# Column sums of a weight, on their way through memory: four small transfers from GpSimd's queue to SyncE's, and the operations around them

## The chip, the core and the metric

One core of one Trainium2 chip runs the whole program. The metric is the device time in microseconds (us) of one launch. Three runs of the kernel before the change gave 235.82, 237.19 and 238.05; the median is 237.19. A profile is one more execution, taken by the hardware profiler; its times are in us from the start of its span unless they are marked ns.

## What is computed

A layer norm of x, then an attention with a sliding dilated window and a gated MLP side by side, all added to x. S = 2048 rows, D = 512, 32 heads of 16, a window of 8 rows at a distance of 2, F = 1792 (two halves of 896).

```python
xn   = layernorm(x)                                  # 2048 x 512
q, k, v = split(xn @ wqkv)                           # 32 heads of 16
logits  = q . k[pos - 2*w] * scale,  w = 0..7        # masked where pos - 2*w < 0
attn    = softmax(logits)
A = (sum over w of attn * v[pos - 2*w]) @ wo
z  = gelu(xn @ w_in)
z1 = z[:, :896];  z2 = layernorm(z[:, 896:])
B  = (z1 * (w_sp @ z2 + b_sp[:, None])) @ w_out
out = x + A + B
```

## The kernel before

x comes in 16 blocks of 128 rows. Each block is normalised on VectorE and transposed by DMA into xnT. TensorE then makes V, Q, K, the second half z2 and the first half z1T of the MLP, later the product of w_sp with z2 (L976, the largest part, in four quarters of 112 matmuls), and at the end the outputs (L1032 with wo, L1041 with w_out). ScalarE moves results out of PSUM, with gelu and exp. VectorE makes the window products of Q and K (L743, with their sums L748), the softmax, the products of the attention with V (the "PV" blocks, L1004 and L1007) and the gate (L987 adds the bias, L990 multiplies).

**The three uncorrected blocks.** To let TensorE start early, V of the blocks 0 to 2 is computed from x that is not centred (`NRAW = 3`). Such a V block needs a correction: minus the mean times rstd, times the column sums of the weight wv. The column sums are made on TensorE with ones (L777, in the step that also reduces the logits of the first two quarters, "red0", L766) and come as four partial sums on four groups of 32 partitions. To add them up and to spread them over 128 partitions they go through memory, in `colsum` (L657 to L672):

- ScalarE copies the partial sums out of PSUM, negated ("cse", L658),
- transfer csa (L660) writes the four rows of 512 to DRAM,
- transfer csb (L662) reads them back, four columns to a partition,
- GpSimd adds them in two steps, csu and csv (L665, L667),
- transfer csc (L669) writes the 512 sums to DRAM,
- transfer csr (L671) reads them into all 128 partitions.

All four transfers are issued by GpSimd. Then VectorE corrects the three blocks (`fix_all`, L753, "the corrections"), and GpSimd's queue stores them to the scratch memory vscr (L686), from which the PV blocks are loaded (L999).

**The order of the work.** Every operation is given to a planner (`Plan.schedule`) with an estimated duration, a priority and what it reads and writes. The planner simulates the engines and fixes each engine's order of instructions. Of the operations that can start within a window of `tol` ns after the first one that can, it takes the one of the highest priority. For some transfers it takes a landing time from a table (`land`) in place of an estimate. Lists of names (L1072 to L1082) pin the order of some operations; a pair of names on one queue fixes which of the two goes first. On the chip each engine runs its list in order and waits at semaphores, so what stands behind a waiting instruction waits as well.

**Space.** Many tensors lie over each other in the arena. Before the change the column sums (ncs) and their partial sums (csp) share one place inside z1T; the raw V blocks (vraw) and the corrected ones (Vn0) lie in z1T as well. A z1 group whose place is still in use is evacuated from PSUM (L882) only when that use is over. The bias of w_sp's product (bbc) shares its place with four slots of V blocks. The third quarter of w_sp's transposes (wT2, L949) lies over the window products, and so waits for the second reduction of the logits ("red2", L766 again).

**Other names in the text.** L789 adds the mask to the logits on VectorE. L849 to L862 normalise z2 in four waves of four blocks; in each, GpSimd takes a power (zr0 to zr3, L859), which VectorE's four L862 wait for. In the order of the lists, zr2 stands behind csa and zr3 behind csr. SyncE loads w_out (L954), wo in four parts (L958; each part waits until the one before it has landed), the bias (L941), and x for the residual (L1022, read by L1047).

Of the kernel before, what the change touches and what calls it, by code (L numbers as in the profile page):

```python
# [9 lines left out]
F32 = mybir.dt.float32  # L10
ALU = mybir.AluOpType
ACTF = mybir.ActivationFunctionType
# [334 lines left out]
def build_kernel(nc, A_x, A_wqkv, A_wo, B_x, B_w_in, B_w_sp, B_b_sp, B_w_out, out, report=False, emit=True):  # L347
    S = A_x.shape[1]
    D = A_x.shape[2]
    assert D == 512 and S % 512 == 0  # L350
    NB = S // 128
# [8 lines left out]
    NRAW = 3  # L360
# [5 lines left out]
    cpart = nc.dram_tensor("cpart", (4, 512), F32).ap()  # L366
    cscr = nc.dram_tensor("cscr", (512,), F32).ap()


    off = {}  # L370
# [19 lines left out]
        place((n + 1) & ~1, **{name: 0})  # L390
    off["xn"] = off["attn"]
    off["xcT"] = off["pb"] + 4096
    off["Vn0"] = off["z1T"] + 1536
    off["ncs"] = off["z1T"] + 3 * S + 1024
    off["vraw"] = off["ncs"] + S
    AR = top[0]
    NWS = 3

    foff = {}
    fb = 0  # L400
    for name, n in (("prime", 4), ("mx", 128), ("Zb", 256), ("Z", 128), ("maskt", 128), ("st6", NB * 6),
                    ("mv", NB * 2), ("vpe", NB), ("rstd", NB), ("s1", NB), ("s2", NB), ("m2", NB), ("msq", NB), ("mr", 4), ("csq", 16), ("css", 4),
                    ("vpe2", NB), ("rstd2", NB), ("mhalf", 4)):
        foff[name] = fb
        fb += n
# [3 lines left out]
    plan = Plan()  # L409

    with ExitStack() as es:
        ar = es.enter_context(nc.sbuf_tensor("arena", [128, AR], BF))
        fp = es.enter_context(nc.sbuf_tensor("fpool", [128, FR], F32))
# [3 lines left out]
        def A(name, n, o2_=0):  # L417
            return ar[:, off[name] + o2_: off[name] + o2_ + n]
# [4 lines left out]
        def Fv(name, n, o2_=0):  # L423
            return fp[:, foff[name] + o2_: foff[name] + o2_ + n]
# [4 lines left out]
        def PC(o_, dims):  # L429
            return bass.AP(tensor=ps, offset=o_, ap=[[PR, 128]] + [list(d) for d in dims])  # L430
# [6 lines left out]
        def R1(key, name, n, o_=0):  # L437
            R(key, "sb", [(off[name] + o_, off[name] + o_ + n)])
# [44 lines left out]
                R1(("xcT", b, hf), "xcT", 256, 512 * b + 256 * hf)  # L483
            R(("xnT", 0, hf), "sb", [(off["xnT"] + dc * S, off["xnT"] + dc * S + 128) for dc in (2 * hf, 2 * hf + 1)])
        R1("ncs", "ncs", 1024)
        for b in range(NRAW):
            R1(("Vn", "raw", b), "Vn0", 512, S * b)
        R1("csp", "ncs", 1024)
        for fc in range(FC):
            for j in range(NJ):  # L490
                R1(("z1T", fc, j), "z1T", 512, fc * S + 512 * j)
# [11 lines left out]
        def c_act(n, psum=True, accum=False):  # L503
            return (170.0 if psum else 205.0) + n * 0.833 + (200.0 if accum else 0.0)
# [7 lines left out]
        T = plan.add  # L512

        def dma(eng, fn, nbytes, chan, reads=(), writes=(), name="", xbar=False, prio=0.0, after=()):
            return T(eng, fn, reads=reads, writes=writes, name=name, prio=prio, after=after,
                     dma=dict(chan=chan, nbytes=nbytes, xbar=xbar, iss=(1270.0 if nbytes < 400000 else 2200.0) if xbar else None))
# [7 lines left out]
        ncs = A("ncs", 1024).bitcast(F32)  # L524
# [5 lines left out]
          writes=["ident"], est=300, name="ident1")  # L530
# [124 lines left out]
            return AC(off["xnT"] + dc * S + 128 * b, [[1, 128]])  # L655

        def colsum(bk):  # L657
            T("act", lambda a: a.activation(ncs.rearrange("p (d h) -> p d h", d=16), PC(bk.col(), [[1, 16], [16, 32]]), ACTF.Copy, scale=-1.0), reads=[bk], writes=["csp"], est=c_act(512),  # L658
              name="cse", prio=-0.5)
            dma("pool", lambda e: e.dma_start(cpart, A("ncs", 1024).bitcast(F32)[0:128:32, :]),  # L660
                8192, "csa", reads=["csp"], writes=["cpart"], name="csa", prio=-5)
            dma("pool", lambda e: e.dma_start(Fv("csq", 16).rearrange("p (q i) -> p q i", q=4),  # L662
                                              bass.AP(tensor=cpart.tensor, offset=cpart.offset, ap=[[4, 128], [512, 4], [1, 4]])),
                8192, "csb", reads=["cpart"], writes=["csq"], name="csb", prio=-5)
            T("pool", lambda g: g.tensor_tensor(Fv("csq", 8), Fv("csq", 8), Fv("csq", 8, 8), ALU.add), writes=["csq"],  # L665
              est=200, name="csu", prio=-5)
            T("pool", lambda g: g.tensor_tensor(Fv("css", 4), Fv("csq", 4), Fv("csq", 4, 4), ALU.add), reads=["csq"],  # L667
              writes=["css"], est=200, name="csv", prio=-5)
            dma("pool", lambda e: e.dma_start(bass.AP(tensor=cscr.tensor, offset=cscr.offset, ap=[[4, 128], [1, 4]]), Fv("css", 4)),  # L669
                2048, "csc", reads=["css"], writes=["cscr"], name="csc", prio=-5)  # L670
            dma("pool", lambda e: e.dma_start(ncs, bass.AP(tensor=cscr.tensor, offset=cscr.offset, ap=[[0, 128], [1, 512]])),  # L671
                128 * 2048, "csr", reads=["cscr"], writes=["ncs"], name="csr", prio=-5)  # L672

        def vraw(b):
            return A("vraw", 1024, S * b).bitcast(F32)
# [13 lines left out]
        def v_block(b):  # L689
            bk = plan.bank("V%d" % b)  # L690
            sl = b % 8
            vk = ("Vn", "raw", b) if b < NRAW else ("Vn", sl)
            vn = A("Vn0", 512, S * b) if b < NRAW else A("Vn" if sl < 4 else "bbc", 512, 512 * (sl % 4))

            for hf in range(2):
                def mm(t, hf=hf):
                    last = None
                    for dc in (2 * hf, 2 * hf + 1):
                        last = t.matmul(P(bk, 512), A("xcT", 128, 512 * b + 128 * dc) if b < NRAW else xTv(b, dc),  # L699
                                        A("wv", 512, 512 * dc), start=(dc == 0), stop=(dc == 3))  # L700
                    return last
                T("pe", mm, reads=[("xcT", b, hf) if b < NRAW else ("xnT", b), ("wv", hf)], writes=[bk],
                  est=2 * c_mm(512) , name="V%d_%d" % (b, hf), prio=(2 if b < 4 else 60 + b))
            vdh = vn.rearrange("p (d h) -> p d h", d=16)
            if b < NRAW:
                T("act", lambda a: a.activation(vraw(b).rearrange("p (d h) -> p d h", d=16), PC(bk.col(), [[1, 16], [16, 32]]), ACTF.Copy,
                                                   scale=Fv("rstd", 1, b)),
                  reads=[bk, ("rstd", b)], writes=[("vraw", b)], est=c_act(512), name="Ve%d" % b, prio=4)
                fixes.append((b, vn, vk))
                return  # L710
            else:
                T("act", lambda a: a.activation(vdh, PC(bk.col(), [[1, 16], [16, 32]]), ACTF.Copy),  # L712
                  reads=[bk], writes=[vk], est=c_act(512), name="Ve%d" % b, prio=4)
            v_write(b, vn, vk)
# [357 lines left out]
        for names in (["warm%d" % wi for wi in range(NWARM)] +  # L1072
                      ["xTx0a", "xTx0b", "warm%d" % NWARM, "V0_0", "xTx1", "V0_1", "xTx2", "V1_0", "V1_1", "xTr0", "V2_0", "V2_1",
                       "z2_0_0", "z2_0_0b", "z2_0_1", "z2_1_0", "z2_1_1", "z2_2_0", "z2_2_1", "V3_0", "V3_1", "z2_3_0", "z2_3_1", "V4_0", "V4_1", "z2_4_0", "z2_4_1", "Q0_0", "Q0_1", "K0_0", "K0_1"],
                      ("rstd7", "Vw3"), ("csr", "Vw0", "Vw1", "Vw2"),
                      ("bnst0", "bnag0", "vpe0", "bnst1", "bnag1", "vpe1", "norm0", "bnst2", "norm1", "bnag2", "vpe2", "bnst3", "norm2",
                       "bnag3", "vpe3", "norm3", "bnst4", "bnag4", "vpe4", "mr", "norm4", "bnst5"),
                      ["bnst%d" % b for b in range(5, NB)],
                      ("xTc0_0", "xTc0_1", "xTc1_0", "xTc1_1", "xTc2_0", "xTe0_0", "xTe0_2", "Ve1", "Ve0", "Ve2",
                       "z2g0", "z2g1", "z2s0"), ("ldx4", "xTd1", "xTd2", "xTd3", "xTd4", "ldq", "ldk", "ldx5", "ldx6", "ldx7", "ldwin1", "ldx8"), ("ldx15", "xTd5"),  # L1080
                      *[("ldwin1", "ldx%d" % b) for b in range(9, NB)], *[("z2_4_1", "%s0_%d" % (n, c)) for n in "QK" for c in range(4)],
                      ("V10_1", "Q3_3"), ("csa", "zr2"), ("csr", "zr3")):  # L1082
            for n0, n1 in zip(names, names[1:]):
                if byname[n0] not in byname[n1].deps:
                    byname[n1].odeps.add(byname[n0])

        plan.schedule(tol=58.0, dma_bw=285.0, dma_lat=1600.0, overlap=60.0,
                      land=dict(ldx0=3600.0, ldwv0=4120.0, ldx1=4550.0, ldwv1=5230.0, ldx2=5600.0, ldwin2a=7650.0, ldx3=6050.0,
                                ldwin2b=8950.0, csa=77000.0, csb=80500.0, csc=83200.0, csr=85900.0, ldx4=9100.0, ldx5=18150.0, ldq=16300.0, xTd3=12130.0, ldk=17800.0, ldx6=18500.0, ldx7=18900.0, xTd4=13900.0, xTd1=9600.0, xTd2=10850.0, ldwin1=21500.0))
        if report:  # L1090
            print("arena", AR, "fp", FR)
            plan.report()
# [48 lines left out]
```

## Time and profile before

| | us |
|---|---|
| median of three runs | 237.19 |
| the profiled execution, its own time | 237.73 |
| its span, first to last instruction | 236.5 |
| ScalarE busy, TensorE's granted clock | 95.9, 1.000 |
| the last L748 on VectorE | 118.82 to 121.11 |
| last matmul ends (L1041) | 234.6 |

The longest waits that concern the change, as the view of waits gives them (who waited, for whom, total, times, longest):

```profile
POOL fpool L665 <- DMA fpool<-cpart: 4.3, 1, 4.3
...
POOL vscr L686 <- DVE arena L753: 3.3, 1, 3.3
...
DVE arena L753 <- DMA arena<-cscr: 2.9, 1, 2.9
...
POOL arena L671 <- DMA cscr<-fpool: 1.4, 1, 1.4
PE ps L766 <- DVE arena L748: 1.4, 1, 1.4
ACT arena L882 <- DVE arena L753: 1.3, 1, 1.3
```

A line of a timeline gives the start, the length, the engine, the line of the kernel, the operation, what it writes and reads with its shape, and how often it stands there in a row. In brackets is the time for which the engine was idle before it, and what ended that. DVE is VectorE, ACT ScalarE, PE TensorE, POOL GpSimd, SP SyncE. A wait is a loss only where the engine that sets the end had nothing else to do; matmuls are pipelined, so the lengths of TensorE's groups overlap a little.

### The profile page before, as it was taken

To read this page: it belongs to the slowest core of one execution; us is meant where nothing else is said; L and a number is where in the kernel's file an instruction comes from. 1 tells how busy PE (TensorE), PEld (TensorE's weight loads), DVE (VectorE), ACT (ScalarE), POOL (GpSimd) and SP (SyncE) were. 2 spreads that over 40 slices of the span, in tenths; PEclk is the share of its full clock that TensorE was granted. 3 is DMA by queue.
4 is the path that set the end of the run, shared out by engine and by line. 5 is a ranking of instruction groups with operands and counts; after the bars stand their busy time and mean duration, and the time that the engine had idled before them with its cause. 6 is when DMAs were issued, how large, how long until landed. Compare 5 with 4: busy or idle time off the path is not lost.

```text
span 236.5 us, 3005 instructions
## 1 busy us (share of the span) xinstructions
PE 232.0 (98%) x1127; PEld 108.3 (46%) x1127; DVE 207.2 (88%) x271; ACT 95.9 (41%) x143; POOL 33.4 (14%) x62
## 2 busy tenths in 40 slices
PE   8999999999999999999979999999999999999996
PEld 3455455544544444444434444444444444444443
DVE  4706999999998987999999999999798999999932
ACT  4798778888986587611010162111111111000000
POOL 2305740504206263000000000000000000000000
DMA  6769935999764523017089999999999692893552
GB/s 198 223 198 369 175 87 117 229 208 186 194 200 144 128 54 103 3 44 215 7 281 276 197 300 237 202 208 314 269 275 244 186 336 56 285 297 81 180 163 67
DMA packets 83823, 44.55 MB, mean 188 GB/s; under 512 B 56060, under 2 KB 83100, under 8 KB 83808
## 3 DMA queue, kind: packets, MB, share of 16 engines
q1 hardware_dynamic: 82400, 41.66, 68.5%
q0 software_dynamic: 976, 2.40, 3.9%
q10 hardware_dynamic: 432, 0.30, 0.4%
q8 instruction: 9, 0.15, 0.3%
q14 instruction: 6, 0.05, 0.1%
HBM read 26.62 MB, written 4.22 MB: 130 GB/s over the span
## 4 chain that ended last, share of the span: by engine, by line
PE 74%; DVE 14%; DMA 8%; issue 2%; POOL 1%; ACT 1%; ACTq 0%
PE ps L976 31%; PE ps L1041 10%; PE ps L830 10%; PE ps L722 9%; PE ps L1032 6%; PE ps L699 5%; DVE arena L748 4%; DVE arena L743 4%; PE ps L876 3%; DMA fpool<-cpart 2%; DMA arena<-cscr 2%; DMA cpart<-arena 1%; DMA arena<-arena 1%; DMA arena<-in_A_x_dram 1%; POOL fpool L667 1%
## 5 line engine op out<-in xcount | busy, mean ns | idle before, releaser
L976 PE MATMUL ps<-arena 128*128 128x512 bf16 x448 | 97.0, 379 | 0.0
L976 PEld LDWEIGHTS ps<-arena 128*128 128x128 bf16 x448 | 43.8, 98 | 53.0 <-issue 0.4
L984 ACT ACTIVATE arena<-ps 128x1024 bf16<-128x1024 f32 (+1 forms) x16 | 14.7, 917 | 80.9 <-PE ps L976 80.9
L743 DVE TENSOR_TENSOR arena<-arena 128x4096 bf16<-128x4096 bf16 x16 | 36.4, 2281 | 0.1
L1004 DVE TENSOR_TENSOR arena<-arena 128x4096 bf16<-128x4096 bf16 x16 | 36.5, 2284 | 0.0
L1007 DVE TENSOR_TENSOR arena<-arena 128x2048 bf16<-128x2048 bf16 (+1 forms) x32 | 30.1, 950 | 0.1
L722 PE MATMUL ps<-arena 128*128 128x512 bf16 x128 | 28.8, 379 | 0.0
L748 DVE TENSOR_TENSOR arena<-arena 128x4096 bf16<-128x4096 bf16 x12 | 27.5, 2288 | 0.1
L1041 PE MATMUL ps<-arena 128*128 128x512 bf16 (+2 forms) x119 | 27.0, 366 | 0.0
L830 PE MATMUL ps<-arena 128*128 128x448 bf16 x128 | 25.9, 353 | 0.2
L876 PE MATMUL ps<-arena 128*128 128x512 bf16 x112 | 24.7, 379 | 0.0
L722 PEld LDWEIGHTS ps<-arena 128*128 128x128 bf16 x128 | 14.4, 113 | 13.3 <-ACT arena L712 0.4
L731 ACT ACTIVATE arena<-ps 128x1024 bf16<-128x1024 f32 x16 | 16.3, 1022 | 6.7 <-PE ps L722 6.4
L830 PEld LDWEIGHTS ps<-arena 128*128 128x128 bf16 x128 | 12.4, 98 | 12.8 <-DMA arena<-in_B_w_in_dram 0.7
L1047 DVE TENSOR_TENSOR arena<-ps,arena 128x512 bf16<-128x512 f32 (+2 forms) x17 | 11.1, 656 | 7.2 <-PE ps L1041 7.1
L1041 PEld LDWEIGHTS ps<-arena 128*128 128x128 bf16 x119 | 11.4, 98 | 12.8
L876 PEld LDWEIGHTS ps<-arena 128*128 128x128 bf16 x112 | 10.9, 98 | 13.4 <-ACT arena L882 0.5
L1032 PE MATMUL ps<-arena 128*128 128x512 bf16 (+2 forms) x68 | 16.6, 366 | 0.0
L838 ACT ACTIVATE arena<-ps 128x896 bf16<-128x896 f32 x16 | 14.6, 913 | 3.9 <-PE ps L830 3.8
L699 PE MATMUL ps<-arena 128*128 128x512 bf16 x64 | 15.9, 379 | 0.2 <-ACT arena L630 0.2
L882 ACT ACTIVATE arena<-ps 128x1024 bf16<-128x1024 f32 (+1 forms) x16 | 13.9, 922 | 4.7 <-PE ps L876 3.4
L622 DVE BATCH_NORM_STATS2 fpool<-arena 128x6 f32<-128x512 bf16 x16 | 10.7, 679 | 5.5 <-DMA arena<-in_A_x_dram 5.5
(68 smaller groups left out, 171.0 us busy)
## 6 DMA issues: line engine op xcount, KB each, us to landing
arena<-vscr SPq DMA_DIRECT2D x16, 1024.0 KB, 6.2
arena<-in_A_x_dram SPq DMA_DIRECT2D x30, 128.0 KB, 4.3
vscr<-arena POOLq DMA_DIRECT2D x16, 128.0 KB, 3.7
out_dram<-arena SPq DMA_DIRECT2D x15, 128.0 KB, 2.0
arena<-in_A_wqkv_dram SPq DMA_DIRECT2D x2, 512.0 KB, 4.6
arena<-in_B_w_in_dram SPq DMA_DIRECT2D x2, 448.0 KB, 5.2
arena<-in_B_w_in_dram SPq DMA_DIRECT2D x1, 896.0 KB, 8.3
arena<-in_B_w_out_dram SPq DMA_DIRECT2D x1, 896.0 KB, 4.9
```

The source lines that it names most:

```text
L699: last = t.matmul(P(bk, 512), A("xcT", 128, 512 * b + 128 * dc) if b < NRAW else xTv(b, dc), A("wv", 512, 512 * dc), start=(dc == 0), stop ...
L722: last = t.matmul(P(bk, 512, 512 * which), AC(off["wqk"] + 2048 * which + 512 * dc + c, [[4, 128]]), AC(off["xnT"] + dc * S + 512 * j, [[1 ...
L731: T("act", lambda a: a.activation(AC(qo, [[ko - qo, 2], [1, 512]]), P(bk, 1024).rearrange("p (t n) -> p t n", t=2), ACTF.Copy, scale=0.5), ...
L743: T("dve", (lambda pbv, qb, kb: lambda v: v.tensor_tensor(pbv, qb, kb, ALU.mult))(pbv, qb, kb), reads=rd, writes=[("pb", s_)], est=c_tt(40 ...
L748: T("dve", (lambda av, bv: lambda v: v.tensor_tensor(av, av, bv, ALU.add))(av, bv), reads=[("pb", 1)], writes=[("pb", acc)], est=c_tt(4096 ...
L830: last = t.matmul(P(bk, 448, 512 * hf), xTv(b, dc), AC(off["w_in2"] + 896 * dc + 448 * hf, [[1, 448]]), start=(dc == 0), stop=(dc == 3))
L876: last = t.matmul(P(bk, 512, 512 * i), AC(off["w_in1"] + 896 * dc + 128 * fc, [[1, 128]]), AC(off["xnT"] + dc * S + 512 * j, [[1, 512]]), ...
L976: last = t.matmul(P(bk, 512, 512 * i), AC(off["z2"] + FH * sh + 128 * fc, [[1, 128]]), AC(off["wT%d" % r_] + sh * 512, [[1, 512]]), start= ...
L1004: T("dve", lambda v: v.tensor_tensor(tv, tv, av, ALU.mult), reads=[("attn", b)], writes=[("Vs", sv)], est=c_tt(4096), name="pv%d" % b, pri ...
L1007: T("dve", (lambda n: lambda v: v.tensor_tensor(A("Vs", n, 4096 * sv), A("Vs", n, 4096 * sv), A("Vs", n, 4096 * sv + n), ALU.add))(n), wri ...
L1032: last = t.matmul(P(bk, cn), AC(off["OT"] + 512 * tb + 128 * cc, [[1, 128]]), AC(off["wo"] + 512 * cc + c0, [[1, cn]]), start=(cc == 0), s ...
L1041: last = t.matmul(P(bk, cn), AC(off["z1T"] + fc * S + 128 * tb, [[1, 128]]), AC(off["w_out"] + 512 * fc + c0, [[1, cn]]), start=False, sto ...
```

## The change

The four transfers are issued by SyncE in place of GpSimd. csb and csc move pieces of 16 floats (64 bytes) on 32 partitions in place of 4 floats (16 bytes) on 128, so the two sums on GpSimd are of 32 and 16 elements on 32 partitions. In the pinned orders, SyncE's load of w_out comes behind csa, csb, csc and csr; the first part of wo and the first load of x for the residual come behind csr; zr3 comes behind csv in place of csr, and zr2 is no longer pinned. The sums now lie in the place of the bias, so the bias is loaded after the corrections. The partial sums keep a place in z1T; the corrected V blocks go to ordinary slots of Vn. The pinned order of the three blocks' stores is dropped. The planner's window is 4 ns in place of 58, and the table has new landing times for the four transfers.

```diff
-    off["Vn0"] = off["z1T"] + 1536
-    off["ncs"] = off["z1T"] + 3 * S + 1024
-    off["vraw"] = off["ncs"] + S
+    off["ncs"] = off["bbc"]
+    off["csp"] = off["z1T"] + 3 * S + 1024
+    off["vraw"] = off["csp"] + S
...
-            dma("pool", lambda e: e.dma_start(cpart, A("ncs", 1024).bitcast(F32)[0:128:32, :]),
+            dma("sp", lambda e: e.dma_start(cpart, A("csp", 1024).bitcast(F32)[0:128:32, :]),
                 8192, "csa", reads=["csp"], writes=["cpart"], name="csa", prio=-5)
-            dma("pool", lambda e: e.dma_start(Fv("csq", 16).rearrange("p (q i) -> p q i", q=4),
-                                              bass.AP(tensor=cpart.tensor, offset=cpart.offset, ap=[[4, 128], [512, 4], [1, 4]])),
+            dma("sp", lambda e: e.dma_start(csv(0, 64).rearrange("p (q i) -> p q i", q=4),
+                                            bass.AP(tensor=cpart.tensor, offset=cpart.offset, ap=[[16, 32], [512, 4], [1, 16]])),
                 8192, "csb", reads=["cpart"], writes=["csq"], name="csb", prio=-5)
-            T("pool", lambda g: g.tensor_tensor(Fv("csq", 8), Fv("csq", 8), Fv("csq", 8, 8), ALU.add), writes=["csq"],
-              est=200, name="csu", prio=-5)
+            T("pool", lambda g: g.tensor_tensor(csv(0, 32), csv(0, 32), csv(32, 32), ALU.add), writes=["csq"],
+              est=1200, name="csu", prio=-5)
...
-            dma("pool", lambda e: e.dma_start(bass.AP(tensor=cscr.tensor, offset=cscr.offset, ap=[[4, 128], [1, 4]]), Fv("css", 4)),
+            dma("sp", lambda e: e.dma_start(bass.AP(tensor=cscr.tensor, offset=cscr.offset, ap=[[16, 32], [1, 16]]), csv(64, 16)),
                 2048, "csc", reads=["css"], writes=["cscr"], name="csc", prio=-5)
-            dma("pool", lambda e: e.dma_start(ncs, bass.AP(tensor=cscr.tensor, offset=cscr.offset, ap=[[0, 128], [1, 512]])),
+            dma("sp", lambda e: e.dma_start(ncs, bass.AP(tensor=cscr.tensor, offset=cscr.offset, ap=[[0, 128], [1, 512]])),
                 128 * 2048, "csr", reads=["cscr"], writes=["ncs"], name="csr", prio=-5)
+
+        def csv(o_, n):
+            return fp[0:32, foff["csq"] + o_:foff["csq"] + o_ + n]
...
-            vk = ("Vn", "raw", b) if b < NRAW else ("Vn", sl)
-            vn = A("Vn0", 512, S * b) if b < NRAW else A("Vn" if sl < 4 else "bbc", 512, 512 * (sl % 4))
+            vk = ("Vn", sl)
+            vn = A("Vn" if sl < 4 else "bbc", 512, 512 * (sl % 4))
...
-                      ("rstd7", "Vw3"), ("csr", "Vw0", "Vw1", "Vw2"),
+                      ("rstd7", "Vw3"),
...
-                      ("V10_1", "Q3_3"), ("csa", "zr2"), ("csr", "zr3")):
+                      ("V10_1", "Q3_3"), ("csa", "csb", "csc", "csr", "ldwout"), ("csr", "ldwo0"), ("csr", "ldxr0"), ("csv", "zr3")):
...
-        plan.schedule(tol=58.0, dma_bw=285.0, dma_lat=1600.0, overlap=60.0,
+        plan.schedule(tol=4.0, dma_bw=285.0, dma_lat=1600.0, overlap=60.0,
...
-                                ldwin2b=8950.0, csa=77000.0, csb=80500.0, csc=83200.0, csr=85900.0, ldx4=9100.0,
+                                ldwin2b=8950.0, csa=75800.0, csb=78400.0, csc=83400.0, csr=86500.0, ldx4=9100.0,
```

More of the change, by code (lines that the diff above doesn't have):

```diff
@@ L401, in build_kernel @@
     for name, n in (("prime", 4), ("mx", 128), ("Zb", 256), ("Z", 128), ("maskt", 128), ("st6", NB * 6),
-                    ("mv", NB * 2), ("vpe", NB), ("rstd", NB), ("s1", NB), ("s2", NB), ("m2", NB), ("msq", NB), ("mr", 4), ("csq", 16), ("css", 4),
+                    ("mv", NB * 2), ("vpe", NB), ("rstd", NB), ("s1", NB), ("s2", NB), ("m2", NB), ("msq", NB), ("mr", 4), ("csq", 64), ("css", 16),
                     ("vpe2", NB), ("rstd2", NB), ("mhalf", 4)):
@@ L485, in build_kernel @@
         R1("ncs", "ncs", 1024)
-        for b in range(NRAW):
-            R1(("Vn", "raw", b), "Vn0", 512, S * b)
-        R1("csp", "ncs", 1024)
+        R1("csp", "csp", 1024)
         for fc in range(FC):
@@ L657, in colsum @@
         def colsum(bk):
-            T("act", lambda a: a.activation(ncs.rearrange("p (d h) -> p d h", d=16), PC(bk.col(), [[1, 16], [16, 32]]), ACTF.Copy, scale=-1.0), reads=[bk], writes=["csp"], est=c_act(512),
+            T("act", lambda a: a.activation(A("csp", 1024).bitcast(F32).rearrange("p (d h) -> p d h", d=16), PC(bk.col(), [[1, 16], [16, 32]]), ACTF.Copy, scale=-1.0), reads=[bk], writes=["csp"], est=c_act(512),
               name="cse", prio=-0.5)
-            dma("pool", lambda e: e.dma_start(cpart, A("ncs", 1024).bitcast(F32)[0:128:32, :]),
+            dma("sp", lambda e: e.dma_start(cpart, A("csp", 1024).bitcast(F32)[0:128:32, :]),
@@ L664, in colsum @@
                 8192, "csb", reads=["cpart"], writes=["csq"], name="csb", prio=-5)
-            T("pool", lambda g: g.tensor_tensor(Fv("csq", 8), Fv("csq", 8), Fv("csq", 8, 8), ALU.add), writes=["csq"],
-              est=200, name="csu", prio=-5)
-            T("pool", lambda g: g.tensor_tensor(Fv("css", 4), Fv("csq", 4), Fv("csq", 4, 4), ALU.add), reads=["csq"],
-              writes=["css"], est=200, name="csv", prio=-5)
-            dma("pool", lambda e: e.dma_start(bass.AP(tensor=cscr.tensor, offset=cscr.offset, ap=[[4, 128], [1, 4]]), Fv("css", 4)),
+            T("pool", lambda g: g.tensor_tensor(csv(0, 32), csv(0, 32), csv(32, 32), ALU.add), writes=["csq"],
+              est=1200, name="csu", prio=-5)
@@ L670, in colsum @@
+            T("pool", lambda g: g.tensor_tensor(csv(64, 16), csv(0, 16), csv(16, 16), ALU.add), reads=["csq"],
+              writes=["css"], est=1200, name="csv", prio=-5)
+            dma("sp", lambda e: e.dma_start(bass.AP(tensor=cscr.tensor, offset=cscr.offset, ap=[[16, 32], [1, 16]]), csv(64, 16)),
                 2048, "csc", reads=["css"], writes=["cscr"], name="csc", prio=-5)
-            dma("pool", lambda e: e.dma_start(ncs, bass.AP(tensor=cscr.tensor, offset=cscr.offset, ap=[[0, 128], [1, 512]])),
+            dma("sp", lambda e: e.dma_start(ncs, bass.AP(tensor=cscr.tensor, offset=cscr.offset, ap=[[0, 128], [1, 512]])),
@@ L1085, in build_kernel @@
                     byname[n1].odeps.add(byname[n0])
-        plan.schedule(tol=58.0, dma_bw=285.0, dma_lat=1600.0, overlap=60.0,
+        plan.schedule(tol=4.0, dma_bw=285.0, dma_lat=1600.0, overlap=60.0,
                       land=dict(ldx0=3600.0, ldwv0=4120.0, ldx1=4550.0, ldwv1=5230.0, ldx2=5600.0, ldwin2a=7650.0, ldx3=6050.0,
-                                ldwin2b=8950.0, csa=77000.0, csb=80500.0, csc=83200.0, csr=85900.0, ldx4=9100.0, ldx5=18150.0, ldq=16300.0, xTd3=12130.0, ldk=17800.0, ldx6=18500.0, ldx7=18900.0, xTd4=13900.0, xTd1=9600.0, xTd2=10850.0, ldwin1=21500.0))
+                                ldwin2b=8950.0, csa=75800.0, csb=78400.0, csc=83400.0, csr=86500.0, ldx4=9100.0, ldx5=18150.0, ldq=16300.0, xTd3=12130.0, ldk=17800.0, ldx6=18500.0, ldx7=18900.0, xTd4=13900.0, xTd1=9600.0, xTd2=10850.0, ldwin1=21500.0))
         if report:
```

## The prediction

> **What bounds the kernel now.** I read the page's first part, then TensorE's timeline, the chain of waits, and the timelines of VectorE, GpSimd and ScalarE around the moved transfers. Part 1 (busy time and share of the span by engine):
>
> ```profile
> PE 232.0 (98%) x1127; PEld 108.3 (46%) x1127; DVE 207.2 (88%) x271; ACT 95.9 (41%) x143; POOL 33.4 (14%) x62
> ```
>
> TensorE is idle for 236.5 - 232.0 = 4.5 us in all: 0.84 before its first matmul, 0.15 in the head, about 1.9 behind its last one (that ends at 234.6), and one gap in the middle. TensorE's timeline, where the bracket is the idle time before a group and who ended it:
>
> ```profile
> 78.84 18.46 PE L876 MATMUL ps<-arena 128*128 128x512 bf16 x84
> 97.13 22.61 PE L976 MATMUL ps<-arena 128*128 128x512 bf16 x104
> 121.16 1.05 PE L766 MATMUL ps<-arena 128*32 128x512 bf16 x16 [1.42 <-DVE arena L748]
> ```
>
> So the gain has a ceiling: 1.42 us of TensorE waiting for VectorE, 0.6% of the time. The rest of VectorE's lateness is free as long as TensorE has matmuls queued. The chain of waits, in order of time (start, length, what), shows why VectorE was late:
>
> ```profile
> 72.40 0.49 ACT arena L658
> 72.90 0.28 issue
> 73.18 3.04 DMA cpart<-arena
> 76.22 0.29 issue
> 76.51 5.02 DMA fpool<-cpart
> ...
> 81.60 0.21 POOL fpool L665
> ...
> 81.89 2.38 POOL fpool L667
> 84.26 0.28 issue
> 84.55 1.70 DMA cscr<-fpool
> 86.25 0.28 issue
> 86.54 3.86 DMA arena<-cscr
> ...
> 90.42 2.08 DVE arena L753 x3
> ```
>
> Four transfers take 3.04 + 5.02 + 1.70 + 3.86 = 13.6 us, the two sums 2.6, handing over from engine to engine 1.3 (90.42 - 72.90 - 13.6 - 2.6). VectorE stands for the corrections (L753):
>
> ```profile
> 85.24 2.29 DVE L748 TENSOR_TENSOR arena<-arena 128x4096 bf16<-128x4096 bf16 x1
> 90.42 2.08 DVE L753 SCALAR_TENSOR_TENSOR arena<-arena,fpool 128x512 bf16<-128x512 f32 x3 [2.90 <-DMA arena<-cscr]
> 92.42 1.79 DVE L862 TENSOR_SCALAR arena<-arena,fpool 128x896 bf16<-128x896 bf16 x4
> ```
>
> From 90.42 to the end of the last L748 at 121.11 VectorE is not idle again, so these 2.90 us, with 0.77 at the mask add (L789, at 72.03), are what TensorE gets back as 1.42.
>
> **The change, part by part.**
>
> *The chain of four on SyncE.* The nearest rows for each step: csa, 8 KB out: ScalarE's 32 KB store landed in 1.5, GpSimd's own csa in 3.0; I take 1.6, as the store is the same kind of queue. csb, 8 KB back: between 1.5 and its own 5.0; loads of 128 KB on the hardware queue at the start took 2.9 and carry sixteen times as much, so I take 2.2. csc, 2 KB out: 1.5 to 1.7, I take 1.6. csr, 256 KB in: 2.9 (half its size, ScalarE's queue) to 3.9 (its own); SyncE's 256 KB loads took 3.5, which I take. The two sums stay on GpSimd with 32 and 16 elements on 32 partitions in place of 8 and 4 on 128. L665 took 0.20, but L667, half its size, 2.37, from 81.89 to 84.26, just as long as VectorE's product of 81.91 ran (2.29). So each is 0.2 or 2.4: 0.4 to 4.8, taken as before, 2.6. Handing over 1.3. Sum: 72.90 + 1.6 + 2.2 + 2.6 + 1.6 + 3.5 + 1.3 = 85.7. Lower end 72.90 + 1.5 + 1.5 + 0.4 + 1.5 + 2.9 + 1.3 = 82.0; upper end, with its own prices and both sums blocked, 72.90 + 13.6 + 4.8 + 1.3 = 92.6. Before: 90.40.
>
> The Trainium skill (SBUF — State Buffer, A bandwidth-pool intuition that's wrong) says that a transfer issued by GpSimd cannot have its descriptors written while VectorE holds the port that the two share, and that one from SyncE is free of this. The trace allows it: csb was issued at 76.51 and VectorE's L748 ran from 76.88 to 79.17; by that rule csb would need 81.53 - 79.17 = 2.4 us, and the sum would come to 85.9.
>
> *The corrections later in VectorE's order.* GpSimd's power for the third normalisation wave (zr2) no longer stands behind csa: its input is ready at 64.3, so its four normalisations (1.78 us, at 79.08) can fill the 0.77 at the mask add. That of the fourth wave (zr3, at 87.10) moves ahead of csc and csr, so its four normalisations (1.71 us net, 92.42 to 94.13) can go before the corrections. VectorE then reaches them at 87.53 - 0.77 + 1.71 = 88.5; if they keep their place, at 86.8. Against 85.7 neither waits. Nothing is added to VectorE: between 71 and 121 it does the same instructions, without 3.67 us of waiting, and the last L748 ends at about 117.4.
>
> What landing time still costs nothing? If the 1.71 moved ahead, a csr at 90.40 + 1.71 = 92.1 brings the last L748 to where it was, and TensorE's 1.42 is gone up to a csr of 90.7. If not moved, the two are 90.4 and 89.0. The planner may also put L766 one group of four matmuls (0.86) earlier in TensorE's order, which tightens each by 0.9: at worst 88.1. The forecast of 85.7 is 2.4 us inside even that.
>
> *SyncE behind the waits.* SyncE now stands from about 73 to 82 for csa, the sums and csc. Behind it: w_out, wo, x for the residual, the bias. SyncE had issued nothing between 64.77 (w_out) and 72.02 (wo), so only these move. w_out, wo and x are first read at 196.4 and 199.0 (L1032, L1047): over 100 us of cover. The bias now also waits for the corrections, as the sums lie in its place; it is read by L987 at 107.48. Everything in sequence from 85: w_out 4.9, four wo at most 3.2 each (they wait for each other), bias 4.7: 107.4 at the very worst. VectorE would be 3.67 earlier, at 103.8, and lose 3.6, no more than it gained; with the bias ahead of the last wo it lands by 101 and costs nothing. Taken: 0.
>
> *The corrected V blocks in Vn.* They go to slots whose stores were issued before 65: no wait. Their own stores (GpSimd, 91.72, 3.7 us) are first needed by the load at 106.99: 11 us of cover. z1's evacuation (L882) waited 1.30 for L753 at 92.59 with TensorE not idle; the partial sums at (fc 3) are now free after csa, so one evacuation of 1.02 more can go before the corrections. Cost 0.
>
> *The narrower planning window (58 to 4 ns)* changes picks among operations that become ready within 54 ns of each other. The delicate one: the product of the first PV block (L1004, 2.29, now at 121.62) may go ahead of the last sums of L748. With its own sums that is 2.29 + 1.13 + 0.60 + 0.33 = 4.35 us; less the 3.67, L766 would be 0.7 later than now, and the planner, which sees this, puts it later among TensorE's matmuls. What hangs on L766 is the third quarter of w_sp (L949, slot wT2): its last transpose issued near 139.0 lands at 144, and TensorE wants it at about 148 (122.1 + 120 matmuls by 0.216). Cover 4 us; cost 0, and 1 us for each us beyond that.
>
> Sum: 237.73 (the profiled execution; span 236.5 and 1.2 around it) - 1.42 = 236.3. The profiled one lies 0.54 above the median of the three runs, 237.19, so in the median 235.8.
>
> **The rivals.**
>
> *The chain gets no shorter.* The trace gives each transfer a flight of 1.7 to 5.0 and no small one on SyncE before; if the flights are in the memory and not the queue, csr lands near 90.4. TensorE then waits 0 to 1.42: 235.8 to 237.2, say 236.5. For it: csc already took 1.70, hardly above the 1.5 of a store. Against it: csb's 5.0 has nothing like it on the hardware queues. The Trainium skill (DMA: Bandwidth & Descriptors, Issuing engines are not separate DMA queues) says that issuing from another engine saves only the sequencer's issue time. By it this rival's 236.5 would be the result; no row here settles it.
>
> *Slower: the sums are late.* Both sums stand out a product of VectorE and the two transfers keep 3.0 and 5.0, or w_out is already in flight beside csr: csr at 92.6 or later. Place: VectorE's wait before L753, then L766, and before it z1's evacuations, which need the buffers that the corrections read, with TensorE out of banks. It decides from 92.1 (corrections behind the normalisations) or 90.4 (not), and costs 1 us per us: at 92.6, 0.5 to 2.2 more than now, 237.7 to 239.4. Over 1% it needs a csr at 92.8 to 94.5.
>
> *Slower: the new order.* Two PV blocks ahead of L766 (8.7 us) would make wT2 late by 8.7 - 3.67 - 4.0 = 1.0, and a worse mix more: 237 to 241.
>
> **How the numbers follow.** Forecast, most of the 1.42 recovered: 0.70, 235.8. No shorter chain: 0.13, 236.5. Sums late: 0.09, 238.5. New order: 0.08, 239. The three runs spread by 1.4 below and 0.9 above the median, so about 1%, 2.4 us, is what can be told from no change. The ceiling of 0.6% allows faster by over 1% only through that spread: 0.08. Slower by over 1% takes half of each slow rival and an unseen stall: 0.16. Within: 0.76. The range takes the forecast with half the spread below it (234.5) and reaches up into the slow rivals (238.8).
>
> **What would show it.** Right: the bracket before L766 gone or under 0.3; csr landed by 87; no bracket before L753; the four L862 ahead of L753; TensorE's busy share up, its idle near 3.1. Wrong: csr later than 90, a bracket with L882 or L976 on TensorE, a bias that VectorE waits for at L987, or a transpose of w_sp that lands after TensorE asks for it.

## The result, and the profile after

| | before | after |
|---|---|---|
| median of 22 runs each, us | 237.68 (235.82 to 239.01) | 235.95 (235.78 to 236.72) |
| ratio, 95% interval | | 0.9933 [0.9917, 0.9949] |
| the profiled execution, its span | 237.73, 236.5 | 236.54, 235.3 |

The changed kernel is 0.7% faster: 1.7 us in the medians, 1.2 to 2.0 by the interval. The spread of the runs has shrunk from 3.2 to 0.9 us, and the fastest run before, 235.82, is as fast as the fastest after, 235.78, so not every run before had the loss that the change removes. In the profiled executions the difference is 1.19, because this execution was 0.47 us late before the first reduction (L766, now L767) already: 71.18 against 70.71. From there to the second reduction, which now stands one group of four matmuls (0.86) earlier, TensorE took 50.45 before and takes 47.93 + 0.86 = 48.79, a gain of 1.66. From the first reduction to the end of the span it is 165.8 before and 164.1 after. (Lines behind the moved code have numbers higher by one.)

Part 1 of the page of the changed kernel:

```profile
PE 232.4 (99%) x1127; PEld 109.0 (46%) x1127; DVE 207.3 (88%) x271; ACT 95.9 (41%) x143; POOL 29.4 (12%) x58
```

TensorE is idle for 235.3 - 232.4 = 2.9 us: 0.2 in the head, the rest at the two ends. Its timeline has no bracket any more where 1.42 stood:

```profile
79.31 18.29 PE L877 MATMUL ps<-arena 128*128 128x512 bf16 x84
97.44 21.75 PE L977 MATMUL ps<-arena 128*128 128x512 bf16 x100
119.11 1.05 PE L767 MATMUL ps<-arena 128*32 128x512 bf16 x16
```

VectorE's timeline of the changed kernel: the four normalisations (L863) now stand ahead of the corrections (L754), which do not wait. The only wait between here and the last L749, which ends at 118.20 in place of 121.11, is 0.94 for a product of TensorE that ScalarE had to move out of PSUM (L985); there VectorE has become the one that is early.

```profile
84.44 1.77 DVE L863 TENSOR_SCALAR arena<-arena,fpool 128x896 bf16<-128x896 bf16 x4
86.13 2.28 DVE L749 TENSOR_TENSOR arena<-arena 128x4096 bf16<-128x4096 bf16 x1
88.33 2.07 DVE L754 SCALAR_TENSOR_TENSOR arena<-arena,fpool 128x512 bf16<-128x512 f32 x3
...
112.51 0.69 DVE L988 TENSOR_TENSOR arena<-arena 128x1024 bf16<-128x1024 bf16 x1 [0.94 <-ACT arena L985]
```

SyncE's timeline, with csa (L658), csb (L660), csc (L667), csr (L669), three loads of x that stand between csb and csc (L1023), and then the first load of x (not shown) and w_out, which were put behind the four:

```profile
73.39 0.66 SPq L658 DMA_DIRECT2D cpart<-arena  x1
75.19 0.35 SPq L660 DMA_DIRECT2D fpool<-cpart  x1
78.64 1.30 SPq L1023 DMA_DIRECT2D arena<-in_A_x_dram  x3
79.99 0.43 SPq L667 DMA_DIRECT2D cscr<-fpool  x1
82.01 0.33 SPq L669 DMA_DIRECT2D arena<-cscr  x1
...
82.86 0.43 SPq L955 DMA_DIRECT2D arena<-in_B_w_out_dram  x1
```

The sums on GpSimd, and from the view of the transfers (size, us from issue to landing) their flights; csa has no figure there, so 1.8 is taken, the time until its successor was issued, an upper bound:

```profile
76.80 0.24 POOL L663 TENSOR_TENSOR fpool<-fpool 32x32 f32<-32x32 f32 x1 [4.02 <-DMA fpool<-cpart]
77.11 0.21 POOL L665 TENSOR_TENSOR fpool<-fpool 32x16 f32<-32x16 f32 x1
```

```profile
arena<-cscr SPq DMA_DIRECT2D x1, 256.0 KB, 3.9
...
fpool<-cpart SPq DMA_DIRECT2D x1, 8.0 KB, 1.5
cscr<-fpool SPq DMA_DIRECT2D x1, 2.0 KB, 2.0
```

Flights of 1.8 + 1.5 + 2.0 + 3.9 = 9.2 in place of 13.6; csr lands at 85.9 in place of 90.40, 2.4 us before VectorE comes to it. The whole 4.4 of difference are csa (3.04 to at most 1.8) and csb (5.02 to 1.5); csc took 2.0 after 1.7, and csr 3.9 as before. csc was also issued 2.6 us after the sums were done: the second, third and fourth load of x were not pinned, went ahead of it on SyncE, and waited until TensorE had read the weights in their place:

```profile
SPq L1023 <- PE ps L723: 3.1, 1, 3.1
```

### The profile page after: what moved, and what is told of

Same layout as the page of the kernel before. It is cut to its first block, busy times and chain, and to the rows that moved or that the text cites. A ratio compares the mean times of both kernels' runs of the same rounds, so it can differ in the third digit from the quotient of the medians.

```text
span 235.3 us, 3002 instructions
## 1 busy us (share of the span) xinstructions
PE 232.4 (99%) x1127; PEld 109.0 (46%) x1127; DVE 207.3 (88%) x271; ACT 95.9 (41%) x143; POOL 29.4 (12%) x58
## 4 chain that ended last, share of the span: by engine, by line
PE 98%; DVE 0%; ACT 0%; issue 0%; DVEq 0%
PE ps L977 41%; PE ps L723 12%; PE ps L831 10%; PE ps L877 10%; PE ps L1042 10%; PE ps L700 6%; PE ps L1033 6%; PE ps L581 1%; PE ps L767 1%; PE ps L600 1%; DVE arena L1048 0%; ACT arena L628 0%; PE ps L778 0%; DVEq L325 0%
## 5 line engine op out<-in xcount | busy, mean ns | idle before, releaser
L977 PE MATMUL ps<-arena 128*128 128x512 bf16 x448 | 97.0, 379 | 0.0
L977 PEld LDWEIGHTS ps<-arena 128*128 128x128 bf16 x448 | 43.8, 98 | 53.0 <-issue 0.4
L985 ACT ACTIVATE arena<-ps 128x1024 bf16<-128x1024 f32 (+1 forms) x16 | 14.7, 917 | 77.0 <-PE ps L977 70.6
L749 DVE TENSOR_TENSOR arena<-arena 128x4096 bf16<-128x4096 bf16 x12 | 27.4, 2287 | 0.1
```

The lines of the kernel that those rows point to most:

```text
L749: T("dve", (lambda av, bv: lambda v: v.tensor_tensor(av, av, bv, ALU.add))(av, bv), reads=[("pb", 1)], writes=[("pb", acc)], est=c_tt(4096 ...
L977: last = t.matmul(P(bk, 512, 512 * i), AC(off["z2"] + FH * sh + 128 * fc, [[1, 128]]), AC(off["wT%d" % r_] + sh * 512, [[1, 512]]), start= ...
```

## The experiments

The theories, by the letters of the expectations. A: all that counts is whether csr has landed when VectorE's fixed order reaches the corrections. B: it is SyncE's queue that makes the chain short. C: it is the new order. D: what waits on SyncE costs elsewhere. E: the window. For the length of csb: P, the pieces of 16 bytes; Q, VectorE holds up GpSimd's queue; L, other loads are in flight.

Each ratio is to the kernel before, run on the same chip in the same job. "csr" is when it landed in the profiled execution (issue plus flight), "wait" VectorE's for the chain (for csr, or for the power zr3 that stands behind the sums), "gap" TensorE's in the same stretch. The kernel before had medians of 237.68, 237.43, 237.18 and 237.56 in the four jobs, so ratios of different jobs differ by some thousandths where the medians agree.

| kernel | median | ratio, 95% interval | csr | wait | gap |
|---|---|---|---|---|---|
| before | 237.68 | 1 | 90.4 | 2.90 | 1.42 |
| after | 235.95 | 0.9933 [0.9917, 0.9949] | 85.9 | 0 | 0 |
| order only | 236.67 | 0.9968 [0.9945, 0.9991] | 90.2 | 0 | 0 |
| queue only | 235.95 | 0.9950 [0.9923, 0.9977] | 85.7 | 0 | 0 |
| after, on GpSimd | 236.20 | 0.9963 [0.9939, 0.9987] | 89.4 | 1.45 | 0 |
| after, window 58 | 235.99 | 0.9949 [0.9924, 0.9973] | 85.6 | 0 | 0 |
| after, csb 3 times more | 235.98 | 0.9955 [0.9936, 0.9973] | 88.6 | 0.17 | 0 |
| after, csb 5 times more | 236.25 | 0.9968 [0.9948, 0.9988] | 89.5 | 1.47 | 0 |
| after, csb 9 times more | 242.71 | 1.0241 [1.0195, 1.0286] | 95.5 | 7.64 | 5.87 |
| after, x behind csr | 236.08 | 0.9951 [0.9928, 0.9975] | 82.2 | 0 | 0 |
| pieces only | 237.24 | 0.9996 [0.9974, 1.0018] | 89.5 | 2.12 | 0.79 |
| order and pieces | 236.20 | 0.9958 [0.9939, 0.9978] | 91.3 | 0.94 | 0.49 |
| loads behind only | 235.94 | 0.9944 [0.9923, 0.9965] | 85.4 | 0 | 0 |
| after, 16-byte pieces | 235.80 | 0.9943 [0.9922, 0.9964] | 86.2 | 0 | 0 |

From the start of the first reduction to the end of the span, the ten profiled executions without a gap (gap 0 in the table) all take 164.1 to 164.2, whatever their queue, order or pieces. The others take longer by about their gap: pieces only 165.0, order and pieces 164.7, nine more 170.2, before 165.8. The first reduction itself starts anywhere between 70.43 and 71.61, and that alone scatters the profiled times of the ten.

**Order only.** The kernel before, with the plan corrected and nothing else.

```diff
-  ("csa", "zr2"), ("csr", "zr3")
+  ("csv", "zr3")
-  csa=77000.0, csb=80500.0, csc=83200.0, csr=85900.0
+  csa=76200.0, csb=81500.0, csc=86300.0, csr=90400.0
```

> The kernel before with its transfers left on GpSimd; only the plan is told the truth: zr2 is not pinned, zr3 stands behind csv, and the table has the landing times that the trace of before showed (76.2, 81.5, 86.3, 90.4). Window 58 ns as before. Theory A (what counts is only whether csr has landed when VectorE's fixed order reaches L753; the queue does not matter by itself): csr lands at 90 to 91.5, VectorE comes there at about 91 after other work, waits under 0.6, the 1.42 us gap of TensorE before L766 is gone, and the time is that of the changed kernel, 236.0 (235.7 to 236.6). Theory B (the gain is the shorter chain on SyncE's queue): 237.5, the gap stays above 1 us.

In the profile the gap is gone with a csr that lands no earlier than before, as A says:

```profile
118.76 1.05 PE L766 MATMUL ps<-arena 128*32 128x512 bf16 x16
```

But the median is 236.67, above the 236.6 that A allowed, and only about half of the gain. The view of ScalarE's waits shows what this order leaves thin: z1's evacuation still waits for the corrections, which now come later (91.10 to 93.17).

```profile
ACT arena L882 <- DVE arena L753: 1.2, 1, 1.2
```

**Queue only.** The kernel before with the four transfers on SyncE in 64-byte pieces, and w_out, wo and the first x pinned behind csr; the corrections stay ahead of the normalisations. The planner's estimate for each sum is 1200 ns in place of 200, as in the changed kernel, and it put some of VectorE's other operations ahead of the corrections in another order.

```diff
-  dma("pool", ...)   # csa, csb, csc, csr
+  dma("sp", ...)     # in 64-byte pieces
+  ("csa", "csb", "csc", "csr", "ldwout"), ("csr", "ldwo0"), ("csr", "ldxr0")
```

> The kernel before with the four transfers on SyncE in 64-byte pieces and SyncE's loads pinned behind them; landing table, pins of zr2 and zr3, window and places as before, so the corrections stay ahead of the fourth wave's normalisations. Theory A: csr lands by 86.5, before VectorE comes to L753 at about 87.5 to 88; no wait there, no gap before L766, 236.0 (235.7 to 236.6). Theory B says the same, 236.0. Theory C (the gain is the new order, not the chain): 237.5 with the gap kept. Rival D (waiting transfers on SyncE hold up the bias or x): a wait of VectorE at L987 and over 237.

The whole gain in the median, though the runs reach from 235.65 to 237.76: the gain does not need the corrections behind the normalisations, and C falls. No engine waited for the bias, x, wo or w_out, so D falls too. The bias was not held back here and went ahead of csb on SyncE (L944 is the bias, L662 csb), and csb's flight was 3.2 in place of 1.5: a first sign that the company counts, on SyncE as well.

```profile
74.86 0.35 SPq L944 DMA_DIRECT2D arena<-in_B_b_sp_dram  x1
75.61 0.33 SPq L662 DMA_DIRECT2D fpool<-cpart  x1
```

**The changed kernel on GpSimd's queue.**

```diff
-  dma("sp", ...)     # csa, csb, csc, csr
+  dma("pool", ...)
-  ("csa", "csb", "csc", "csr", "ldwout")
+  ("csa", "csb", "csc", "csr"), ("csr", "ldwout")
```

> The changed kernel with the four transfers back on GpSimd, 64-byte pieces kept; the order of TensorE, ScalarE and VectorE is that of the changed kernel. Theory A: the chain is again some 3 to 6 us longer than the plan believes; csv ends at 82 to 84.3, zr3 (behind it) at 83.5 to 87, csr lands at 90 to 93.5. VectorE waits before the fourth wave's L863 and before L754, 1.7 to 5.2 us in all; 0.9 of slack before L767 and 0.9 at L988 take 1.8 of it, so a gap of 0 to 3.4 before L767, most likely 1.4: 237.4 (236.0 to 239.4). Theory C (the order makes the gain): 236.0, no gap.

Here SyncE's loads stood behind nothing, but the plan put them at 78 and later. csa took 1.7 and csb 1.9, on GpSimd's queue and with no load of SyncE in flight; csc, issued at 80.50 after four loads of x, the one of w_out and the first of wo (from 77.95), took 4.8.

```profile
cpart<-arena POOLq DMA_DIRECT2D x1, 8.0 KB, 1.7
fpool<-cpart POOLq DMA_DIRECT2D x1, 8.0 KB, 1.9
cscr<-fpool POOLq DMA_DIRECT2D x1, 2.0 KB, 4.8
```

So csa and csb were short on GpSimd's queue too where they were without loads, which speaks against B; csr landed 3.5 later than in the changed kernel, which the kernel with the loads behind has to settle. My size was off for that reason: VectorE waited 1.45, less than the 1.8 of cover, and TensorE nothing.

```profile
89.44 2.08 DVE L754 SCALAR_TENSOR_TENSOR arena<-arena,fpool 128x512 bf16<-128x512 f32 x3 [1.45 <-DMA arena<-cscr]
```

**The window alone**, 4 back to 58 ns, in the changed kernel:

> The changed kernel with the planner's window back at 58 ns. TensorE's order is the same. Theories A, B: no effect, 236.0 (within 0.3 of the changed kernel), no gap before L767. Theory E (part of the gain, or of the narrower spread of the runs, comes from the window): over 0.4 us slower.

235.99: no effect, E falls.

**A longer chain in the changed kernel.** csb is done again 3, 5 or 9 times, with the order of every engine unchanged.

```diff
+  for k in range(3):   # 5, 9
+      dma("sp", ..., name="csb%d" % k)    # csb once more
```

> The changed kernel with csb done three times more, one after the other; every engine's order is otherwise the same. Each repeat costs 1.6 us, so the sums start at 81.6 in place of 76.8. In the changed kernel csc stands 2.6 us behind three loads of x on SyncE after the sums are done; that wait now takes 2.6 of the 4.8. csr lands at 88.1 in place of 85.9, VectorE comes to L754 at 88.33: no wait, no gap, no change (235.95, within 0.3). Rival (any lengthening of the chain costs, since SyncE is held): 1 to 2 us slower.

> The changed kernel with csb done five times more. Sums at 84.85, csr at 91.3. VectorE waits 3.0 in all (before the fourth wave's L863, since zr3 stands behind csv, and before L754). 0.9 at L767 and 0.9 at L988 absorb 1.8 of it: a gap of 1.2 before L767, 237.1 (236.5 to 237.8). Rival (TensorE runs out of banks before L767, because L883 waits for the corrections): a gap with L877 already here and a larger loss.

> The changed kernel with csb done nine times more. Sums at 91.3, csr at 97.8. VectorE waits about 9.4 in all, TensorE loses 9.4 - 1.8 = 7.6: first with L877, as L883 waits for the corrections until about 100 and TensorE is out of banks from about 94 to 95, the rest before L767. 243.5 (242 to 245). Rival (only L767 matters and z1's evacuations do not): the same sum, but no gap with L877.

Three more cost nothing, as expected. Five more were to cost 1.2 and cost 0.3 in the median and nothing in the profile: the sums began at 83.87, not 84.85, csr landed at 89.5, and the wait of 1.47 stayed under the cover. Nine more cost 6.8 in the median, where 7.6 was expected. VectorE's wait was 7.64, not 9.4, since the sums began at 90.11 in place of 91.3. With five and nine more VectorE waited for zr3, which stands behind the second sum, ahead of the fourth wave's normalisations (L867 here); when it came to the corrections, csr was there. TensorE's timeline shows where the wait came through, first in z1 (L881), where ScalarE could not empty the banks, then before the second reduction (L771):

```profile
91.68 1.78 DVE L867 TENSOR_SCALAR arena<-arena,fpool 128x896 bf16<-128x896 bf16 x4 [7.64 <-POOL fpool L864]
```

```profile
98.09 1.90 PE L881 MATMUL ps<-arena 128*128 128x512 bf16 x8 [2.88 <-ACT arena L887]
...
124.56 1.05 PE L771 MATMUL ps<-arena 128*32 128x512 bf16 x16 [2.99 <-DVE arena L753]
```

2.88 + 2.99 = 5.87 of 7.64: cover 1.77, against 1.8 expected.

**All of x behind csr**, so that csc need not stand behind it:

```diff
-  ("csr", "ldxr0")
+  ("csr", "ldxr0"), ("csr", "ldxr1"), ("csr", "ldxr2"), ("csr", "ldxr3")
```

> The changed kernel with all four loads of x for the residual pinned behind csr, not the first alone. csc is then issued as soon as the sums are done (77.4 in place of 80.0) and csr lands 2.6 earlier, at 83.3. Theory A: VectorE comes to L754 at 88.33 all the same, no change in time (235.95, within 0.3). Rival (the chain's length is still what sets the time): up to 1 us faster.

csr landed 3.7 us earlier, and the time did not move: beyond the point where VectorE comes late anyway, a shorter chain is worth nothing.

**Pieces only, and the order with pieces.** csb's 5.0 us were still unexplained. In the kernel before, and in the order-only kernel, csb and csc in 64-byte pieces:

```diff
-  ap=[[4, 128], [512, 4], [1, 4]]      # csb; csc likewise
+  ap=[[16, 32], [512, 4], [1, 16]]
```

> The kernel before with csb and csc in 64-byte pieces on 32 partitions and the sums on 32 partitions; queue (GpSimd), places, pins, window, landing table and the order of every engine as before. Theory P (csb's 5.0 us are its 512 pieces of 16 bytes): csb lands in 1.7 to 2.5, csr by 86 to 88, VectorE waits under 0.5 before L753, no gap before L766, 236.0 (235.7 to 236.6). Theory Q (csb is long since GpSimd's queue is held by VectorE's two-input operations or since other loads are in flight): csb stays at 4 to 5, the gap stays at 1 to 1.4, 237.4.

> The order-only kernel with 64-byte pieces too; every engine's order is that of the order-only kernel, whose median is 236.67 though its profiled execution shows no gap. If its last 0.7 us are runs in which csr lands late, and theory P holds, csr lands at 86 to 88 and the median is 236.0 (235.7 to 236.3). If they have another cause in that order, 236.6 again.

The pieces alone gave nothing in the median (0.9996). In the profile csb took 3.6, which lies between what P and Q had given, and csa and csc now took over 3:

```profile
cpart<-arena POOLq DMA_DIRECT2D x1, 8.0 KB, 3.5
fpool<-cpart POOLq DMA_DIRECT2D x1, 8.0 KB, 3.6
cscr<-fpool POOLq DMA_DIRECT2D x1, 2.0 KB, 3.1
```

With the order it came to 236.20, between the two values expected; csr landed at 91.3, not at 86 to 88 as P had it. Its profiled execution, at 237.12 one of its longer ones, shows the loss that the order-only kernel's did not: TensorE out of banks in z1, while ScalarE waits for the corrections. (VectorE's 0.94 in the table is a wait for zr3.)

```profile
94.53 3.63 PE L879 MATMUL ps<-arena 128*128 128x512 bf16 x16 [0.49 <-ACT arena L885]
```

That this is also what the order-only kernel loses in its median is likely, but no profile of that kernel shows it.

**Loads behind only.** The kernel before, 16-byte pieces, GpSimd's queue, old order, old landing table; SyncE merely holds wo, x and the bias until csr has landed.

```diff
+  ("ldwo0", "ldbbc"), *[("ldwo0", "ldxr%d" % b) for b in range(4)]
+  byname["ldwo0"].deps.add(byname["csr"])
```

> The kernel before (16-byte pieces, GpSimd's queue, old order of the corrections) with SyncE's loads of wo, the bias and x held until csr has landed, so that no load is in flight beside the four transfers. Theory L (the loads lengthen the chain): csb at 2 to 3.5, csr at 87 to 89, gap under 0.5, 236.2 (235.8 to 236.8). Theories P and Q (pieces, or VectorE): csb at 4.4 to 5.0, the gap stays, 237.2 or more.

235.94: the whole gain, with the runs as close together (0.6 us) as those of the changed kernel. From 60 to 123 us TensorE and VectorE do the same operations in the same order as before. What differs is SyncE. Before, it issued two parts of wo (L958), the bias (L941) and x (L1022) beside csa (73.18 to 76.22) and csb (76.51 to 81.53):

```profile
72.02 0.73 SPq L958 DMA_DIRECT2D arena<-in_A_wo_dram  x1
74.15 0.35 SPq L941 DMA_DIRECT2D arena<-in_B_b_sp_dram  x1
76.05 0.57 SPq L958 DMA_DIRECT2D arena<-in_A_wo_dram  x1
78.17 1.76 SPq L1022 DMA_DIRECT2D arena<-in_A_x_dram  x4
```

Here its first load comes when csr has landed:

```profile
85.44 0.72 SPq L958 DMA_DIRECT2D arena<-in_A_wo_dram  x1
```

The four flights are 9.4 in place of 13.6, VectorE comes to the corrections without a wait, and TensorE's gap before L766 is gone:

```profile
arena<-cscr POOLq DMA_DIRECT2D x1, 256.0 KB, 3.7
...
cpart<-arena POOLq DMA_DIRECT2D x1, 8.0 KB, 1.7
fpool<-cpart POOLq DMA_DIRECT2D x1, 8.0 KB, 2.3
cscr<-fpool POOLq DMA_DIRECT2D x1, 2.0 KB, 1.7
```

```profile
87.16 2.08 DVE L753 SCALAR_TENSOR_TENSOR arena<-arena,fpool 128x512 bf16<-128x512 f32 x3
```

```profile
119.24 1.05 PE L766 MATMUL ps<-arena 128*32 128x512 bf16 x16
```

L holds, and B falls: queue, pieces and order are those of before. The cleanest pair is csa: in both kernels GpSimd issued it 0.95 us after the start of the same product of VectorE (L743), and it took 3.0 with the loads and 1.7 without. For csb a share of Q stays open, as it was issued 0.37 us ahead of a product of VectorE (L748) before, and 1.5 us ahead of it here.

**16-byte pieces on SyncE**, in the changed kernel (the last diff but one, the other way round):

> The changed kernel with csb and csc in 16-byte pieces on 128 partitions, on SyncE; orders as in the changed kernel. Theory P: csb lands in 4 to 5 us in place of 1.5, the sums start at about 79.5 to 80, csc is issued at 80 to 82.5, csr lands at 86 to 88.3; VectorE waits under 0.5 and nothing is lost: 236.0 (235.7 to 236.4). Theory Q or L: csb stays at 1.5 to 2.2, 236.0 too. The time tells nothing here, csb's flight does.

csb took 1.9 where the 64-byte pieces of the changed kernel and of its variants took 1.5 to 1.7: without loads beside them the pieces are worth 0.2 to 0.4 us, and P falls as the cause of 5.0.

```profile
fpool<-cpart SPq DMA_DIRECT2D x1, 8.0 KB, 1.9
```

## Why the prediction was right, point by point

**The ceiling and the sum.** The prediction took away TensorE's 1.42 and nothing else. Measured: 1.73 between the medians, 1.66 between the two reductions of the profiles. Right in place and sign; 0.16 of the rest is z1's stretch, which became that much tighter (from the first reduction to the first L977 26.26 in place of 26.42). That the median came so close to 235.8 is in part luck: the prediction took off 0.54 because the profiled execution lay that far above the median of three runs, but over 22 runs the median before is 237.68, and the same sum would give 236.3.

**The chain.** 85.7 was forecast, 85.9 came. The sum was right because errors cancel, which is luck. The sums on GpSimd took 0.5, not 2.6: they met VectorE's L795, which reads PSUM, and not a product with two inputs from SBUF. Handing over took about 0.2, not 1.3 (csa's 1.8 has its own in it). Against these, csc stood 2.6 behind the loads of x: the prediction counted all of x among what comes behind csr, but only the first load is pinned there. The flights were 9.2 where 8.9 was taken, and this execution started the chain 0.5 later. The time did not hang on the sum: with csr at 89.4 and 89.5 (on GpSimd, and csb five times more) the profiles show no loss, which fits the 89.8 that follows from the prediction's 90.7 less the 0.9 for L766's earlier place.

**Its reason.** The step that failed is the one by which the flights were priced: rows of hardware queues in place of GpSimd's. SyncE as the issuer is not what makes them short: with the loads held back GpSimd's take 9.4 in place of 13.6, and SyncE's with nothing beside them (all of x behind csr) at most 8.3, so the loads are worth about 4 us and queue and pieces together about 1. The change shortens csa and csb because on SyncE the loads that flew beside them now come later. csc took 2.0 right behind three loads of x, so not every load costs as much; which of them do was not tried one by one, nor were the four transfers on SyncE with the loads left beside them. The Trainium skill (DMA: Bandwidth & Descriptors, Issuing engines are not separate DMA queues) says that transfers of all issuing engines run on the same engines and interleave. The runs agree: GpSimd's csa took 3.0 with SyncE's loads beside it and 1.7 without. So that rule does not speak against the change, as the rival had it; it fits what the runs show as its cause. The rival itself (no shorter chain) did not come, since it overlooked that SyncE's order keeps the loads away. The other way to the sum, by which csb waits out VectorE's L748, is not borne out either: on GpSimd's queue without loads csb was issued inside such a product and landed in 1.9.

**VectorE.** Corrections at 88.5 forecast, 88.33 measured; the four normalisations ahead of them; the 0.77 at the mask add filled; L767 one group earlier. All seen. The last L749 ended at 118.20, where 117.4 was forecast: before it VectorE waited 0.94 for TensorE's result (L988), which the forecast did not have, and TensorE's 0.47 of lateness in this execution is part of that.

**What was costed at nothing.** The bias was issued at 90.48, landed 4.2 later, and no L988 waited for it; w_out, wo, x cost nothing; the window nothing; the order of PV and L767 did not change. The transposes of w_sp were not late.

**The slow rival.** Its price held, its condition did not come: it was to be slower than before from a csr of 92.1 on. Of 7.64 us of wait 1.77 were absorbed, and z1's banks and the second reduction were the places, as it said, though VectorE's own wait stood ahead of the fourth wave's normalisations, for zr3.

## What to carry to other kernels

A chain of small dependent transfers can pay for the large loads that are in flight beside it: before moving it to another queue or reshaping its pieces, hold the loads that nobody needs yet until it is through. Work out from the engine that sets the end how late such a chain may land, with the cover on each engine between, since earlier than that is worth nothing, and later cost TensorE one for one here. Where an order is fixed from estimated landings, a landing that is off by 4.5 us (85.9 in the table, 90.4 in the trace) is itself a loss; correcting the table and the pins of the two powers recovered about half in the median.

## What the runs showed of the hardware

- Transfers of 2 and 8 KB took 1.3 to 2.3 us with no load of SyncE beside them, on either queue. The two of 8 KB took 3.0 to 5.0 beside parts of wo (128 KB), the bias (512 KB) and x, and 3.2 on SyncE right behind the bias. The one of 2 KB took 1.7 to 3.1 on GpSimd after loads of wo and x, 4.8 after x, w_out (896 KB) and wo, and 1.3 to 2.0 on SyncE right behind three loads of x.
- A small sum on GpSimd took 0.2 to 0.4 us, or up to 2.4 where it met a product of VectorE. In the kernel with csb three times more, the second sum took 2.16 while such a product ran, the first 0.24. The Trainium skill (SBUF — State Buffer, SBUF: two separate sides) says that a VectorE operation with two inputs from SBUF and GpSimd lock each other out for a whole instruction; the traces agree.
- The Trainium skill (SBUF — State Buffer, Who interferes with whom) says that GpSimd's transfers are held up by VectorE's operations in two-port modes, and that a tensor_tensor was not seen to hold them up. The products here are TENSOR_TENSOR, and the run agrees: with no load beside it, csb on GpSimd landed in 1.9 though it was issued inside a product of VectorE (74.93, the product from 74.02 to 76.30). Whether VectorE adds to a flight that has loads beside it was not tried apart.
